# Reordering the first attention of a fused gated-attention and expert kernel, with the weight loads ahead, the state update later and each later gate two units ahead of its use

## The chip, the cores and the metric

One core of one Trainium2 chip. In the profiles PE is TensorE (PEld its weight loads), DVE is VectorE, ACT ScalarE, POOL GpSimd and SP SyncE; L142 is line 142 of the kernel. The metric is the device time of one execution in microseconds (us), median of several executions. The mean granted TensorE clock is recorded with each: I call span x granted clock the *full-clock time*. It is a calculation (it treats all time at half clock as half lost).

## The reference

```python
# gated linear attention: B=4, H=8, S=768, D=48
f = sigmoid(f_logit)
for t in range(S):
    state = f[t][:, None] * state + outer(k[t], v[t])
    y[t] = q[t] @ state
# then four experts for all tokens, x = y as (3072, 384)
p = domain_probs / domain_probs.sum(-1)
out = sum(p[:, e] * (relu(x @ w1[e]) @ w2[e]) for e in range(4))   # w1: 384x1024, w2: 1024x384
```

## The kernel before

The sequence is cut into 6 chunks of 128 steps. A chunk's attention, for 4 batches, runs `gate` (ACT), `pe_cs` (cumulative sums on TensorE), `exps` (ACT, then q and k products on DVE and POOL), `pe_tp`/`ev_tp` (transposes and copy), `pe_at`/`ev_at` (scores and mask), `pe_y`/`ev_y`, `pe_kv`/`ev_kv`/`state` (the recurrent state for the next chunk) and `pe_xt`/`ev_xt` (the experts' input). The expert work is cut into *units*: `mm_h`, three matmuls of the first product (L286), and `mm_o`, four of the second (L302). Chunk c+1's attention is issued between chunk c's units; chunk 0's has nothing beside it. Each engine takes its instructions in program order, and the program order is what the author writes.

```python
gate(0, 0)
plan = staggered(attention_plan(0))        # steps of batch b at 5*b + s
nw = [(0, 1), (1, 1), (0, 2), (2, 1), (1, 2), (3, 1), (2, 2), (3, 2)]   # (expert, w1 or w2)
for s in sorted(plan):
    if s == 5: gate(0, 1)
    if s == 10:
        w_ins.append(load_w(*nw.pop(0)))   # POOL's queue; casts to bf16
        after(w_ins[0], kB)
    run_steps(plan[s])                     # PE part of a step, then its ACT/DVE/POOL part
for w in nw:                               # seven loads behind all of POOL's work
    w_ins.append(load_w(*w))
...
def state(c, b):                           # on POOL
    for r in range(2):
        nc.gpsimd.tensor_tensor(out=Sf[ps, b], in0=Sf[ps, b], in1=eg, op=ALU.mult)
        nc.gpsimd.tensor_copy(out=nb[ps, b, :, r * D:(r + 1) * D], in_=Sf[ps, b])
...
# inside chunk c >= 1: attention of chunk c+1, at these units
base = 4 if c > 1 else 20
for s, x in staggered(plan).items():
    steps.setdefault(base + s - 4, []).extend(x)
for half in range(2):                      # the gate stands at the same unit as the first sums
    steps.setdefault(base - 4 + half, []).insert(0, ([lambda half=half: gate(c + 1, half)], []))
```

## Time and profile before

| | before |
|---|---|
| median of 3 executions | 352.21 us (350.58 to 352.37) |
| profiled span, granted clock | 354.0 us, 0.975 |
| TensorE / DVE / ACT / POOL busy | 89 / 45 / 42 / 27 % |
| first expert matmul | 30.18 us |
| first second-product matmul | 42.03 us |

The page's view of the span in 40 slices of 8.9 us; each digit is a busy share or a clock in tenths:

```profile
PE   0677599988785999989999989999899999999995
PEclk9999989999697899999999999999999999999999
DMA  9962999999896049004069011000011000010002
```

TensorE is full from the sixth slice on but for a dent at 71 to 115 us (digits 8, 8, 7, 8, 5). The clock row dips in the sixth, eleventh, thirteenth and fourteenth slice. The transfer engines are busy until 115 us, but TensorE names a transfer as its reason for waiting only near 38 and 42 us. The rest is in the prediction.

### The profile page before, as it was taken

Reading aid. Unit: us, or ns where it says so; the run is one execution under the profiler, and the core shown is the slowest. Engines: PE = TensorE matmul, PEld = TensorE weight load, DVE = VectorE, ACT = ScalarE, POOL = GpSimd, SP = SyncE. Lnnn points to the kernel's source line nnn. Section 1 sums busy time; section 2 is a strip of 40 time slices with the busy share of each in tenths; the row PEclk is TensorE's granted clock in tenths of the full one; section 3 lists DMA queues with packets and bytes.
Section 4 is the critical chain, followed back from the end, with each engine's and each line's share of the span. In section 5 each row is a group of like instructions: output and inputs, shape, how many; then the busy total and the mean of one; then the engine's idle time right before and its main releaser. Section 6 shows DMA issues by size and latency. Waiting matters only on the chain.

```text
span 354.0 us, 5713 instructions
## 1 busy us (share of the span) xinstructions
PE 313.7 (89%) x2272; PEld 184.4 (52%) x2304; DVE 161.0 (45%) x259; ACT 149.0 (42%) x295; POOL 96.2 (27%) x164
## 2 busy tenths in 40 slices
PE   0677599988785999989999989999899999999995
PEld 0563245555463765545665545665455555555553
DVE  4574123437071466535456435456353463432343
ACT  4433243252546553373553464533455534234320
POOL 4458100053514471122441122442134300000000
PEclk9999989999697899999999999999999999999999
DMA  9962999999896049004069011000011000010002
GB/s 176 184 92 38 208 206 193 218 208 224 206 224 106 0 96 215 4 22 107 8 131 183 0 45 46 2 0 2 1 50 42 3 0 2 22 67 2 0 2 89
DMA packets 111403, 30.31 MB, mean 86 GB/s; under 512 B 102672, under 2 KB 109840, under 8 KB 111376
## 3 DMA queue, kind: packets, MB, share of 16 engines
q1 hardware_dynamic: 105616, 23.65, 34.4%
q0 software_dynamic: 5760, 6.29, 10.8%
q8 instruction: 18, 0.29, 0.3%
q14 instruction: 9, 0.07, 0.1%
HBM read 31.51 MB, written 4.72 MB: 102 GB/s over the span
## 4 chain that ended last, share of the span: by engine, by line
PE 78%; ACT 6%; DMA 4%; DVE 3%; POOL 3%; issue 3%; SPq 1%; ACTq 0%; POOLq 0%; DVEq 0%
PE op L302 34%; PE hp L286 32%; PE pt L176 3%; DMA w_sb<-in_moe_w_dram 3%; PE A L194 2%; ACT gp L135 2%; ACT ex L133 2%; DMA fg<-in_f_logit_dram 2%; PE pt L229 2%; DVE AT L200 1%; PE pt L142 1%; PE pt L215 1%; POOL kp L164 1%; ACT h_sb L294 1%; PE pt L255 1%
## 5 line engine op out<-in xcount | busy, mean ns | idle before, releaser
L286 PE MATMUL hp<-xT,w_sb 128*128 128x512 bf16 (+1 forms) x592 | 159.9, 374 | 6.4 <-ACT xT L261 1.7
L302 PE MATMUL op<-w_sb,h_sb 128*128 128x384 bf16 x768 | 156.4, 329 | 3.3 <-DMA w_sb<-in_moe_w_dram 3.1
L294 ACT ACTIVATE h_sb<-hp 128x512 bf16<-128x512 f32 (+1 forms) x130 | 73.3, 564 | 133.2 <-PE hp L286 125.2
L302 PEld LDWEIGHTS <-h_sb 128*128 128x128 bf16 x768 | 75.2, 99 | 70.5 <-issue 5.1
L292 DVE TENSOR_SCALAR h_sb<-hp 128x512 bf16<-128x512 f32 (+1 forms) x78 | 50.7, 650 | 81.9 <-PE hp L286 80.0
L286 PEld LDWEIGHTS <-w_sb 128*128 128x128 bf16 x624 | 58.3, 101 | 50.0 <-issue 11.3
L312 DVE SCALAR_TENSOR_TENSOR o_sb<-op,pn,o_sb 128x384 f32<-128x384 f32 x72 | 44.4, 617 | 64.1 <-PE op L302 56.4
L162 POOL TENSOR_TENSOR qp<-qg,eQ 128x384 bf16<-128x384 f32 x20 | 20.0, 998 | 120.6 <-ACT eQ L153 89.2
L247 POOL TENSOR_TENSOR Sf<-Sf,egs 48x192 f32<-48x192 f32 x40 | 20.1, 502 | 52.6 <-DVE Sf L239 50.9
L200 DVE TENSOR_TENSOR AT<-A,mask 128x1024 bf16<-128x1024 f32 x24 | 29.3, 1222 | 3.0 <-PE A L194 2.4
L164 POOL TENSOR_TENSOR kp<-kg,eK 128x384 bf16<-128x384 f32 x24 | 24.7, 1030 | 10.1 <-ACT egs L159 10.1
L239 DVE TENSOR_TENSOR Sf<-Sf,pt 48x192 f32<-48x192 f32 x40 | 14.0, 351 | 22.6 <-PE pt L229 19.6
L142 PE MATMUL pt<-gp,Ub 128*128 128x384 bf16 x24 | 9.0, 374 | 15.3 <-ACT gp L135 15.3
L309 ACT ACTIVATE o_sb<-op,pn 128x384 f32<-128x384 f32 x24 | 14.0, 584 | 15.5 <-PE op L302 14.8
L183 DVE COPY QK<-pt 112x1024 bf16<-112x1024 bf16 x24 | 16.5, 689 | 8.5 <-PE pt L176 8.5
L221 ACT CAST yb<-pt 128x384 bf16<-128x384 f32 x24 | 11.6, 483 | 15.9 <-PE pt L215 15.6
L153 ACT ACTIVATE eQ<-pt 128x384 f32<-128x384 f32 x24 | 11.7, 488 | 12.9 <-PE pt L145 11.9
L261 ACT COPY xT<-pt 128x384 bf16<-128x384 bf16 x24 | 11.4, 477 | 12.7 <-PE pt L255 12.7
L145 PEld LDWEIGHTS <-gp 128*112 128x112 bf16 x80 | 8.9, 158 | 14.5 <-issue 12.8
L248 POOL CAST sb<-Sf 48x192 bf16<-48x192 f32 x40 | 13.6, 340 | 2.6
L215 PE MATMUL pt<-vb,AT 128*128 128x48 bf16 x192 | 11.9, 190 | 2.5 <-DVE AT L200 1.3
L176 PE MATMUL pt<-ident,qp 128*112 128x128 bf16 x96 | 10.6, 240 | 3.5 <-DVE qp L162 2.5
(45 smaller groups left out, 179.4 us busy)
## 6 DMA issues: line engine op xcount, KB each, us to landing
w_sb<-in_moe_w_dram POOLq DMA_DIRECT2D x8, 768.0 KB, 14.2
fg<-in_f_logit_dram SPq DMA_DIRECT2D x12, 384.0 KB, 5.8
kg<-in_k_dram SPq DMA_DIRECT2D x12, 384.0 KB, 5.6
qg<-in_q_dram SPq DMA_DIRECT2D x12, 384.0 KB, 5.8
vg<-in_v_dram SPq DMA_DIRECT2D x12, 384.0 KB, 5.6
out_dram<-o_sb SPq DMA_DIRECT2D x24, 192.0 KB, 1.9
pt<-in_moe_domain_probs_dram SPq DMA_DIRECT2D x1, 48.0 KB, 9.9
```

What stands on the lines that cost most here:

```text
L162: lead.tensor_tensor(out=Qpad[c % NB][:, b, :, 0:D], in0=t["q"][:, bs, :], in1=eQ.rearrange("t (h d) -> t h d", d=D), op=ALU.mult)
L164: nc.gpsimd.tensor_tensor(out=Kpad[c % NB][:, b, :, 0:D], in0=t["k"][:, bs, :], in1=eK.rearrange("t (h d) -> t h d", d=D), op=ALU.mult)
L176: nc.tensor.transpose(out=tp[:, j, i, :], in_=src[:, b, 2 * i:2 * i + 2, :].rearrange("t h d -> t (h d)")[:, 0:MP], identity=ident)
L183: nc.vector.tensor_copy(out=QK, in_=t["tp", b])
L200: nc.vector.tensor_tensor(out=AT.rearrange("s r i t -> s (r i t)"), in0=t["A", b].rearrange("s r i t -> s (r i t)"), in1=mask01, op=ALU.mult)
L215: nc.tensor.matmul(out=y[:, h * D:(h + 1) * D], lhsT=AT[:, r, i, :], rhs=vb[:, h, :], start=(c == 0), stop=True, skip_group_check=True)
L247: nc.gpsimd.tensor_tensor(out=Sf[ps, b], in0=Sf[ps, b], in1=eg, op=ALU.mult)
L286: nc.tensor.matmul(out=hp[:, n0:n1], lhsT=w1_sb[:, e, kk, fc * 128:(fc + 1) * 128], rhs=t["xT"][:, kk, n0:n1], start=(kk == 0), stop=(kk = ...
L292: nc.vector.tensor_relu(out=hs[:, fc, n0:n1], in_=hp[:, n0:n1])
L294: nc.scalar.activation(out=hs[:, fc, n0:n1], in_=hp[:, n0:n1], func=AF.Relu)
L302: nc.tensor.matmul(out=op, lhsT=t["h", e][:, fc, nt * T:(nt + 1) * T], rhs=w2_sb[:, e, fc, :], start=(fc == 0), stop=(fc == KF - 1))
L312: nc.vector.scalar_tensor_tensor(out=o, in0=op, scalar=pe, in1=o, op0=ALU.mult, op1=ALU.add)
```

## The change

It means to shorten the one attention that has nothing beside it (steps issued batch by batch in the order in which a pipeline would run them, inputs loaded by quarter), to have the weights in place in time (all eight on POOL's queue right behind its last key product), to keep chunk 0's state update off that path (issued at expert units 3, 5, 7 and 9), and to leave two units between a later chunk's gate and its first use. Small moves in PSUM, where TensorE's results go, come with it (chunk 0's sums and expert-input transposes take banks that the experts use later).

```diff
-    load(0, 0, "fkq")
-    load(0, 1, "f")
...
+    for x in "f0 k0 q0 f1 f2 k1 q1 v0 f3 k2 q2 v1 k3 q3 v2 v3".split():
+        ins = load(0, x[0], int(x[1]), int(x[1]) + 1)
...
-            if c < C - 1:
+            if 0 < c < C - 1:
                 pe.append(lambda b=b: pe_kv(c, b))
...
+    def first_attention():
+        for b in range(B):
+            for at, f in ((0.0, gate), (1.2, pe_cs), (1.8, exps), (3.0, products), (4.2, pe_tp),   # (abridged)
+                          (5.4, ev_tp), (6.2, pe_at), (6.9, ev_at), (7.0, cast_v), (8.2, pe_y),
+                          (8.8, ev_y), (9.4, pe_xt), (10.0, ev_xt)):
+                ops.append((3.6 * b + at, b, f))
+            if b == B - 1:
+                ops.append((3.6 * b + 4.1, b, weights))
+        for at, b, f in sorted(ops, key=lambda x: x[:2]):
+            f()
...
-                        steps.setdefault(min(30 + 2 * i + b, n), []).append(plan[b, s])
+                        steps.setdefault(min(31 + 2 * i + b, n), []).append(plan[b, s])
+                for b in range(B):
+                    steps.setdefault(3 + 2 * b, []).append(
+                        ([lambda b=b: pe_kv(0, b)], [lambda b=b: ev_kv(0, b), lambda b=b: state(0, b)]))
...
-                base = 4 if c > 1 else 20
+                base = 2 if c > 1 else 18
-                    steps.setdefault(base + s - 4, []).extend(x)
+                    steps.setdefault(base + s, []).extend(x)
```

More of the change, by code (lines that the diff above doesn't have):

```diff
@@ L61, with load @@
     cur = {}
-    def load(c, half, names):
+    def load(c, names, b0, b1):
         t = cur.setdefault(c, {})
@@ L68, in load @@
                 t[nm] = io.tile([T, B * H, D], FP32, name=nm + "g")
-            hs = slice(half * 16, half * 16 + 16)
+            hs = slice(b0 * H, b1 * H)
             ins.append(nc.sync.dma_start(out=t[nm][:, hs, :], in_=srcs[nm][c, :, hs, :]))
@@ L76, in after @@
                           reason="order of transfers")
-    load(0, 0, "fkq")
-    load(0, 1, "f")
-    load(0, 0, "v")
-    kB = load(0, 1, "kqv")[0]
+    for x in "f0 k0 q0 f1 f2 k1 q1 v0 f3 k2 q2 v1 k3 q3 v2 v3".split():
+        ins = load(0, x[0], int(x[1]), int(x[1]) + 1)
+        if x == "k3":
+            k_last = ins[0]
     pt = const.tile([128, B * C, E], FP32)
@@ L125, in load_w, with bank, gate @@
         return nc.gpsimd.dma_start(out=w2_sb[:, e], in_=w2_r[e])
-    def gate(c, half):
+    def bank(c, kind, shape, dtype):
+        if c == 0 and kind == "cs":
+            return ps_h.tile(shape, dtype, name="hp")
+        if c == 0 and kind == "xp":
+            return ps_o.tile(shape, dtype, name="op")
+        return ps_t.tile(shape, dtype, name="pt")
+    def gate(c, b0, b1):
         t = cur[c]
-        hs = slice(half * 16, half * 16 + 16)
-        ex = wk.tile([T, 16, D], FP32, name="ex")
+        hs = slice(b0 * H, b1 * H)
+        ex = wk.tile([T, 16, D], FP32, name="ex")[:, 0:(b1 - b0) * H]
         nc.scalar.activation(out=ex, in_=t["f"][:, hs, :], func=AF.Exp, scale=-1.0)
@@ L139, in pe_cs @@
         g = Gpad[c % NB]
-        cs = ps_t.tile([T, 512], FP32, name="pt")
+        cs = bank(c, "cs", [T, 512], FP32)
         t["cs", b] = cs
@@ L155, in exps @@
         nc.scalar.activation(out=eK, in_=cs[:, 0:HD], func=AF.Exp)
+        t["e", b] = (eQ, eK)
         if c < C - 1:
@@ L159, in exps, with products @@
             nc.scalar.activation(out=t["egs"][:, b, :], in_=cs[0:MP, HD:HD + NP], func=AF.Exp, scale=-1.0)
+    def products(c, b):
+        t = cur[c]
+        eQ, eK = t["e", b]
         bs = slice(b * H, b * H + H)
@@ L165, in exps, with cast_v @@
                                 in1=eK.rearrange("t (h d) -> t h d", d=D), op=ALU.mult)
-        vb = wk.tile([T, H, D], BF16, name="vb")
+    def cast_v(c, b):
+        t = cur[c]
+        bs = slice(b * H, b * H + H)
+        lead = nc.vector if c == 0 else nc.gpsimd
+        vb = wk.tile([T, H, D], BF16, name="vb", bufs=5)
         lead.tensor_copy(out=vb, in_=t["v"][:, bs, :])
@@ L171, in pe_tp @@
         t = cur[c]
-        tp = ps_t.tile([MP, 2, NP, T], BF16, name="pt")
+        tp = bank(c, "tp", [MP, 2, NP, T], BF16)
         t["tp", b] = tp
@@ L205, in pe_y @@
         t = cur[c]
-        y = ps_t.tile([T, 512], FP32, name="pt")
+        y = bank(c, "y", [T, 512], FP32)
         t["y", b] = y
@@ L225, in pe_kv @@
         t = cur[c]
-        KV = ps_t.tile([T, 512], FP32, name="pt")
+        KV = bank(c, "KV", [T, 512], FP32)
         t["KV", b] = KV
@@ L251, in pe_xt @@
         t = cur[c]
-        xp = ps_t.tile([T, KD, T], BF16, name="pt")
+        xp = bank(c, "xp", [T, KD, T], BF16)
         t["xp", b] = xp
@@ L269, in attention_plan @@
             o = 0
-            put(o, [lambda b=b: pe_cs(c, b)], [lambda b=b: exps(c, b)])
+            put(o, [lambda b=b: pe_cs(c, b)], [lambda b=b: exps(c, b), lambda b=b: products(c, b), lambda b=b: cast_v(c, b)])
             put(o + 4, [lambda b=b: pe_tp(c, b)], [lambda b=b: ev_tp(c, b)])
@@ L361, in run_steps, with weights @@
                 x()
-    gate(0, 0)
-    plan = staggered(attention_plan(0))
-    nw = [(0, 1), (1, 1), (0, 2), (2, 1), (1, 2), (3, 1), (2, 2), (3, 2)]
-    w_ins = []
-    for s in sorted(plan):
-        if s == 5:
-            gate(0, 1)
-        if s == 10:
-            w_ins.append(load_w(*nw.pop(0)))
-            after(w_ins[0], kB)
-        run_steps(plan[s])
-    for w in nw:
-        w_ins.append(load_w(*w))
+    def first_attention():
+        ops = []
+        for b in range(B):
+            for at, f in ((0.0, lambda b=b: gate(0, b, b + 1)), (1.2, lambda b=b: pe_cs(0, b)),
+                          (1.8, lambda b=b: exps(0, b)), (3.0, lambda b=b: products(0, b)),
+                          (4.2, lambda b=b: pe_tp(0, b)), (5.4, lambda b=b: ev_tp(0, b)),
+                          (6.2, lambda b=b: pe_at(0, b)), (6.9, lambda b=b: ev_at(0, b)),
+                          (7.0, lambda b=b: cast_v(0, b)), (8.2, lambda b=b: pe_y(0, b)),
+                          (8.8, lambda b=b: ev_y(0, b)), (9.4, lambda b=b: pe_xt(0, b)),
+                          (10.0, lambda b=b: ev_xt(0, b))):
+                ops.append((3.6 * b + at, b, f))
[3 more added lines that the diff above has]
+            f()
+    w_ins = []
+    def weights():
+        for w in ((0, 1), (1, 1), (0, 2), (2, 1), (1, 2), (3, 1), (2, 2), (3, 2)):
+            w_ins.append(load_w(*w))
+        after(w_ins[0], k_last)
+    first_attention()
     pn = const.tile([128, B * C, E], FP32)
@@ L382 @@
     nc.vector.tensor_tensor(out=pn, in0=pt, in1=psm.broadcast_to([128, B * C, E]), op=ALU.mult)
-    l1 = load(1, 0, "fkqv")
+    l1 = load(1, "fkqv", 0, 2)
     after(l1[0], w_ins[5])
-    load(1, 1, "fkqv")
-    load(2, 0, "fqkv")
-    load(2, 1, "fqkv")
+    load(1, "fkqv", 2, 4)
+    load(2, "fkqv", 0, 2)
+    load(2, "fkqv", 2, 4)
     for c in range(C):
@@ L400 @@
                     for b in (0, 1):
-                        steps.setdefault(min(30 + 2 * i + b, n), []).append(plan[b, s])
-                steps.setdefault(29, []).append(([lambda: gate(1, 0)], []))
+                        steps.setdefault(min(31 + 2 * i + b, n), []).append(plan[b, s])
+                steps.setdefault(29, []).append(([lambda: gate(1, 0, 2)], []))
+                for b in range(B):
+                    steps.setdefault(3 + 2 * b, []).append(
+                        ([lambda b=b: pe_kv(0, b)], [lambda b=b: ev_kv(0, b), lambda b=b: state(0, b)]))
             else:
-                base = 4 if c > 1 else 20
+                base = 2 if c > 1 else 18
                 for s, x in staggered(plan).items():
-                    steps.setdefault(base + s - 4, []).extend(x)
+                    steps.setdefault(base + s, []).extend(x)
                 for half in range(2):
-                    steps.setdefault(base - 4 + half, []).insert(0, ([lambda half=half: gate(c + 1, half)], []))
+                    steps.setdefault(base - 2 + half, []).insert(
+                        0, ([lambda half=half: gate(c + 1, 2 * half, 2 * half + 2)], []))
             if c == 1:
@@ L413 @@
                         steps.setdefault(min(at + b - 2, 15), []).append(plan[b, s])
-                steps.setdefault(2, []).append(([lambda: gate(1, 1)], []))
+                steps.setdefault(2, []).append(([lambda: gate(1, 2, 4)], []))
         for i, (h, o) in enumerate(us):
             if i == 0 and 1 <= c and c + 2 < C:
-                load(c + 2, 0, "fqkv")
-                load(c + 2, 1, "fqkv")
+                load(c + 2, "fkqv", 0, 2)
+                load(c + 2, "fkqv", 2, 4)
             if h:
```

## The prediction

> **What bounds the kernel now.** I read the page first. TensorE (PE) is 89% busy, and the chain that ended last is 78% PE (34% line L302, the second expert product; 32% L286, the first), so most of the span is a saturated PE and only its idle stretches can be won. The busy table by stretches, cut where the stages change, says where these are:
>
> ```profile
> core 0: us, PE busy (x) PEld busy (x) DVE busy (x) ACT busy (x) POOL busy (x), PEclk, DMA share, GB/s
> 0.00:30.18 30.18, 14.93 (x145) 11.95 (x145) 18.31 (x35) 11.99 (x25) 14.83 (x31) 1.00 0.85 132
> 30.18:42.03 11.85, 7.65 (x27) 2.82 (x27) 2.90 (x5) 3.58 (x6) 6.84 (x10) 1.00 0.89 144
> 42.03:72.90 30.87, 30.71 (x155) 15.94 (x158) 10.16 (x16) 11.20 (x19) 0.00 (x0) 0.94 1.21 207
> 72.90:86.92 14.02, 11.57 (x121) 7.45 (x119) 8.33 (x14) 4.73 (x12) 7.30 (x13) 1.00 1.20 215
> 86.92:126.36 39.44, 31.58 (x288) 22.80 (x288) 14.65 (x27) 21.15 (x51) 17.43 (x28) 0.83 0.69 130
> 126.36:354.04 227.68, 217.26 (x1541) 123.41 (x1568) 106.66 (x164) 96.35 (x184) 49.84 (x84) 1.00 0.19 44
> ```
>
> The first attention takes 30.18 us before the first expert matmul, with no engine full (PE 14.9, DVE 18.3, POOL 14.8): a latency chain. Then PE works 7.65 of 11.85 us. The later loss is small per us. The chain of waits around the second row says what holds it:
>
> ```profile
> 28.94 0.36 DVE Sf L239
> ...
> 30.44 0.51 POOL Sf L247
> 30.96 0.05 issue
> 31.01 0.34 POOL sb L248
> 31.35 0.74 POOL w_sb L124
> 32.09 9.89 DMA w_sb<-in_moe_w_dram
> 41.99 0.04 issue
> 42.03 0.81 PE op L302 x4
> ```
>
> Seven of the eight weight loads stand on POOL's in-order queue behind the last batch's state update (L247, L248); they are issued from 31.3 us, and the first L302 matmul waits until 42.03. PE's own waits after 30.18 us:
>
> ```profile
> PE pt L142 <- ACT gp L135: 9.1, 6, 2.1
> PE op L302 <- DMA w_sb<-in_moe_w_dram: 3.1, 1, 3.1
> PE hp L286 <- ACT xT L261: 1.7, 3, 0.6
> ```
>
> The largest, 9.1 us in six pieces, is not in the first attention: it is the cumulative-sum matmul (L142) of a later chunk, issued right behind its gate (L133, L135 on ACT). Three of them, 1.69 us each at 153.9, 205.3 and 256.7 us in the timeline, are the only PE waits the view names after 120 us. Last, the half-clock stretches:
>
> ```profile
> 42.85:46.26 3.41, 3.41 (x10) 1.37 (x9) 0.69 (x1) 0.58 (x1) 0.00 (x0) 0.50 1.17 206
> 90.63:97.46 6.83, 6.32 (x33) 4.20 (x32) 0.85 (x2) 2.95 (x10) 4.76 (x6) 0.50 0.76 199
> 111.11:117.94 6.83, 5.47 (x36) 3.78 (x36) 1.55 (x4) 4.05 (x11) 3.43 (x5) 0.50 0.28 58
> ```
>
> The PEclk column is 0.50: each follows a stretch in which PE stood idle a lot.
>
> **What the Trainium skill says.** (1) "TensorE: Matmul & The Clock Gate", Part 1: the array's clock is halved after an idle window of about 3.4 us and restored after a busy one, and windows run free of the program. The trace agrees: the slow stretches are 3.41 and 6.83 us, one and two such windows, behind windows with at most about half of PE busy (1.65 of 3.43 us before 90.63, 1.20 of 3.40 before 111.11). (2) Same page, "Architectural detail": ACT, DVE and POOL queues are strict FIFO. The trace agrees: weight loads 2 to 8, with nothing of their own to wait for, are issued only after the last L248. (3) "DMA: Bandwidth & Descriptors", "Issuing engines are not separate DMA queues": loads from SP and POOL share the same 16 engines. The trace agrees: the chunk-1 loads, beside the last two weights, took 11.2 us to land against 5.8 in the median. (4) "SBUF — State Buffer", "Who interferes with whom": DVE and POOL share a port pair, the loser blocks. One L164 product took 1.80 us beside DVE work against 1.0 usually; I allow for some of this.
>
> **The change, part by part.**
>
> *Loads by batch.* 384 KB halves land 1.8 us apart (8.3, 10.1, 11.9 us ...), so 192 KB quarters should land 0.9 us apart: f0 at about 3.5 instead of 4.4, the last k at 14.3, the last v at 17.0. The bytes are the same. Gain about 0.9 us at the start.
>
> *First attention step by step.* I walk it through in-order queues in the new order with the trace's durations: gate 1.0 us per batch (two of 0.49), L142+L145 0.85, each exp 0.49, qp 0.7, kp 1.0, transposes 1.1, QK copy 0.69, A 0.61, mask product 1.23, v cast 0.36, y 0.50, yb 0.49, xT transposes 0.50, xT copy 0.48. One batch alone takes nearly 10 us. ACT needs 3.1 us per batch and DVE 3.0 (3.7 with the state's 0.73, now gone), but order waits between them spread the batches to about 4.2 us. The walk gives gates ending at 4.5, 7.5, 11.0 and 15.8, kp of the last batch at 19.6, and the last xT at 26.7. **First L286 at about 26.8 instead of 30.18: -3.4 us.**
>
> *Weights.* They now stand on POOL right after that kp: issued from 19.6 to 26.4 us (8 x 0.85). The first load of an idle queue took 6.8 us (31.3 to 38.1), then one landed every 3.85 us (38.1, 42.0, 45.7, 49.5, 53.2). So w1[0] lands at 26.4, in time (it is issued later than before, 14.4, and landed at 22.7, so this slack is spent), w1[1] 30.2, w2[0] 34.1, w1[2] 38.0. PE: 24 L286 matmuls from 26.8, about 3.4 us of them at half clock (0.43 us each, then 0.22), are 6.9 us; the state's key-value products, now among them, 4 x 0.25 us more; one further group of 0.65. First L302 at about 35.2, after w2[0]. **The waits for weights, 3.1 + 0.7 us, vanish, and the half clock at 42.85, which costs 3.41/2 = 1.7 us, has no cause any more.** The first L302 moves from 42.03 to 35.2, 6.8 us, and with the clock the end of that stage is about 8.5 us earlier. I take -8.2 for small waits on the hp buffers, since the deferred adds give DVE 4 x 0.73 us just there.
>
> *Later attention 2 units after its gate instead of at it.* A unit is 1.30 us (one L286 group and one L302 half), so two cover the gate's 1.7 us: 3 x 1.69 = **-5.1 us**, taken as -4.8. In chunk 1 the units at that place are half-width L286 alone (0.33 us each) and ACT has two gates (3.4 us) anyway: PE then runs into the hp buffers that ACT must clear, so of 2.08 us there I give only -1.0.
>
> *Chunk 0 to 1.* The first two batches' steps start one unit later (31 for 30). The chain from their L142 at 73.4 to the first L286 of chunk 1 at 86.9 is 13.5 us of latency (POOL products 4 x 1.0 + 2 x 0.5, then the masks one after the other), and one unit less stands beside it: +1.3 less the 0.34 us of gate wait gone, **about +0.7**. The inputs follow the weights, so they move 9 us earlier too, and the loads do not become the limit.
>
> Sum: -8.2 - 4.8 - 1.0 + 0.7 = -13.3 us. From 352.2 that is 338.9. The half clock at 90.6 and 111.1 costs up to 3.4 us each; the first has its cause unchanged, the second may go or move (I give it one chance in three: -1.1). **Predicted 338 us.**
>
> **Rivals.** (a) *The weights become the wait at the start.* w1[0] has 0.4 us of slack by the estimate. If POOL writes its load commands slowly beside DVE, or the last inputs and the tiny probability load overlap it, PE waits 1 to 3 us at 26.8 and again at w2[0]: 339 to 342. Against it: the loads took 0.74 to 0.93 us to issue in every case. (b) *The pipeline of the first attention does not shorten*, because in-order queues block each other (A has one buffer, ACT has 11 instructions per batch): the start stays near 30 us, but the weights are still 11 us ahead, so the stall and the clock loss still go: about 341. (c) *The gate wait only changes its name*: ACT is no faster, and PE waits for relu results instead (as at 113.27 us, 1.30 us on L294). In full-width chunks ACT ends gate 2 about 3.5 us after gate 1 begins, just as PE comes to need the buffer; if half is given back: 340.5. (d) *The clock decides*: with fewer idle stretches both later slow stretches vanish: 333; if phases fall badly: 342.
>
> **Range and chances.** The three gains (start 3.4, weights and clock 5, gates 5) come from separate mechanisms, each seen as a wait in the trace; for a change under 2% (above 345.2) two of the three would have to fail. The errors: start +-2, weights +-2, clock +-3, gates +-2, together about +-5. Range 332 to 344; faster 0.95, same 0.05, slower under 0.01.
>
> **What would show it.** First L286 near 26.8 us and the weight issues near 19.6 to 26.4; no PE wait on w_sb over 1 us; no half clock between 35 and 60 us; the wait of L142 on L135 down from 9.1 us to under 4, with none after 120 us; the stretch from the chunk-1 L142 to its first L286 still about 13.5 us. The prediction is wrong if PE waits for L294 or w_sb as much as it did for L135 and w_sb before, or if the first L286 stays at 30 us.

## The result, and the profile after

The changed kernel takes **338.66 us** (336.81 to 339.08, 4 executions) against 352.29 us (350.58 to 356.76, 4 executions) for the kernel before. The ratio is 0.9618, 95% interval 0.9572 to 0.9665 (a ratio is the mean time of one kernel's fast runs over that of the other's of the same rounds, so not quite the ratio of the medians quoted). The predicted 338 was 0.7 us off.

In the changed kernel the first product is L304, the second L320, the sums L150, the gate L141 and L143. Its stretches, cut at the same events as the prediction's first table (columns as there: length, busy us of TensorE matmul, weight load, DVE, ACT, POOL, then clock, transfer share, GB/s), with the stretch after the first second-product matmul cut at the start of the sums of chunk 1:

```profile
core 0: us, PE busy (x) PEld busy (x) DVE busy (x) ACT busy (x) POOL busy (x), PEclk, DMA share, GB/s
0.00:25.10 25.10, 13.80 (x129) 10.01 (x129) 15.67 (x29) 12.61 (x29) 14.34 (x24) 1.00 0.92 164
25.10:33.51 8.41, 8.36 (x40) 3.81 (x41) 4.00 (x9) 2.99 (x5) 2.89 (x7) 1.00 1.21 207
33.51:64.19 30.68, 30.68 (x170) 16.38 (x169) 11.32 (x19) 12.71 (x21) 3.85 (x10) 1.00 1.22 209
64.19:77.72 13.53, 10.63 (x115) 6.71 (x113) 8.01 (x13) 3.88 (x11) 6.99 (x12) 1.00 1.20 210
77.72:112.17 34.45, 26.98 (x274) 20.04 (x274) 13.39 (x26) 20.49 (x50) 16.19 (x26) 0.95 0.78 148
112.17:335.10 222.93, 219.04 (x1582) 124.26 (x1581) 107.07 (x165) 95.98 (x185) 51.54 (x88) 1.00 0.20 45
```

The first stretch is 5.1 us shorter. The second is 3.4 us shorter, and TensorE now works 8.36 of its 8.41 us: the weight stall is gone. From the first second-product matmul to chunk 1's first expert matmul it is 44.2 us (33.51 to 77.72) against 44.9 (42.03 to 86.92). Chunk 1 takes 34.5 us against 39.4, the rest 222.9 against 227.7. These sum to 18.9 us, more than the medians differ, because the profiled execution of the kernel before had a clock of 0.975 and that of the changed one 0.995, the best of its five. Chunk 1 shows it: the delay behind the gate is worth 0.8 of its 5.0 us (below), and most of the rest goes with the slow stretch at 90.63, which has no counterpart here. With the same chunk-1 code, the run "weights alone" below lacks that stretch and takes 36.59 us (82.39 to 118.98) where the kernel before takes 39.44.

The chain around the start, in order of time (start, us, what):

```profile
18.23 6.82 DMA w_sb<-in_moe_w_dram
25.05 0.05 issue
25.10 4.43 PE hp L304 x12
```

The first weight still ends the wait, as before the third one did; but the timeline has the last copy of the experts' input end at 24.87, so this costs only 0.2 us. TensorE's waits after 26 us:

```profile
PE pt L150 <- ACT gp L143: 2.8, 2, 1.6
PE A L212 <- DVE AT L218: 1.6, 2, 0.9
PE hp L304 <- ACT xT L279: 1.1, 2, 0.6
```

The wait on the gate has fallen from 9.1 to 2.8 us, and the same view from 120 us on names no wait at all.

### The profile page after: what moved, and what is told of

Its sections match the earlier page's. It is cut to its first block, busy times and chain, and to the rows that moved or that the text cites. A ratio compares the mean times of both kernels' runs of the same rounds, so it can differ in the third digit from the quotient of the medians.

```text
span 335.1 us, 5754 instructions
## 1 busy us (share of the span) xinstructions
PE 309.5 (92%) x2304; PEld 181.2 (54%) x2304; DVE 159.5 (48%) x259; ACT 148.7 (44%) x299; POOL 95.8 (29%) x164
## 4 chain that ended last, share of the span: by engine, by line
PE 86%; ACT 4%; DMA 3%; DVE 3%; POOL 3%; issue 1%; POOLq 0%; DVEq 0%; ACTq 0%
PE hp L304 38%; PE op L320 36%; PE pt L194 3%; DMA w_sb<-in_moe_w_dram 2%; PE A L212 2%; POOL kp L177 2%; PE pt L247 1%; PE pt L233 1%; PE pt L229 1%; PE pt L150 1%; PE pt L273 1%; ACT eQ L161 1%; DVE Sf L257 1%; ACT ex L141 1%; DMA fg<-in_f_logit_dram 1%
## 5 line engine op out<-in xcount | busy, mean ns | idle before, releaser
L304 PE MATMUL hp<-xT,w_sb 128*128 128x512 bf16 (+1 forms) x624 | 159.5, 368 | 4.4 <-ACT xT L279 1.1
L320 PE MATMUL op<-w_sb,h_sb 128*128 128x384 bf16 x768 | 154.9, 326 | 0.0
L320 PEld LDWEIGHTS <-h_sb 128*128 128x128 bf16 x768 | 74.7, 98 | 65.9
L304 PEld LDWEIGHTS <-w_sb 128*128 128x128 bf16 x624 | 57.0, 100 | 45.3 <-issue 7.2
L201 DVE COPY QK<-pt 112x1024 bf16<-112x1024 bf16 x24 | 16.6, 690 | 21.8 <-PE pt L194 21.8
L257 DVE TENSOR_TENSOR Sf<-Sf,pt 48x192 f32<-48x192 f32 x40 | 14.1, 352 | 15.4 <-PE pt L247 14.6
L279 ACT COPY xT<-pt 128x384 bf16<-128x384 bf16 x20 | 9.5, 477 | 22.5 <-PE pt L273 22.5
L161 ACT ACTIVATE eQ<-pt 128x384 f32<-128x384 f32 x20 | 9.8, 490 | 15.4 <-PE pt L153 11.6
L194 PEld LDWEIGHTS <-qp 128*112 128x112 bf16 x96 | 9.4, 146 | 5.8 <-DVE qp L175 2.9
L194 PE MATMUL pt<-ident,kp 128*112 128x128 bf16 x96 | 10.8, 241 | 1.8 <-POOL kp L177 1.8
```

The costliest lines, as they stand in the source:

```text
L194: nc.tensor.transpose(out=tp[:, j, i, :], in_=src[:, b, 2 * i:2 * i + 2, :].rearrange("t h d -> t (h d)")[:, 0:MP], identity=ident)
L201: nc.vector.tensor_copy(out=QK, in_=t["tp", b])
L257: nc.vector.tensor_tensor(out=Sf[ps, b], in0=Sf[ps, b], in1=KV[ps, :, r, :], op=ALU.add)
L304: nc.tensor.matmul(out=hp[:, n0:n1], lhsT=w1_sb[:, e, kk, fc * 128:(fc + 1) * 128], rhs=t["xT"][:, kk, n0:n1], start=(kk == 0), stop=(kk = ...
L320: nc.tensor.matmul(out=op, lhsT=t["h", e][:, fc, nt * T:(nt + 1) * T], rhs=w2_sb[:, e, fc, :], start=(fc == 0), stop=(fc == KF - 1))
```

## The experiments

Eleven kernels and the changed one once more, all correct. The kernel before ran beside each group: its medians were 355.83 to 355.93 us on these chips, not 352, with a granted clock of 0.966 to 0.984. Its 21 executions in three groups span 352.1 to 357.2 us, but their full-clock time only 343.4 to 345.5, mean 344.8. The changed kernel's is 333.0 to 333.7, mean 333.4, in its first five executions. So I compare full-clock times ("full" below) beside medians. No 95% interval of a ratio below is wider than 0.0095 either way, and all lie below 1.

Full-clock time has two limits. It leaves in the slow first matmuls of the expert stage, at which PEclk says 1.00: the first twelve take 4.43 us in one profiled execution of the changed kernel and 5.10 in the other, so 0.37 to 0.43 us each, against 0.24 right after (1.46 for six). And it overrates half clock: of these two executions one has 3.4 us of it in chunk 1, the other 6.8, yet chunk 1 takes 34.45 and 34.92 us. So differences under about 1 us are better read from a stage. The last stage, from chunk 1's first full-width expert matmul on, is 222.9 us in all ten profiled runs with the delay and 227.7 in all four without.

### The delay behind the gate

**Undone in the changed kernel:**

```diff
-                base = 2 if c > 1 else 18
+                base = 0 if c > 1 else 16
...
-                    steps.setdefault(base - 2 + half, []).insert(
+                    steps.setdefault(base + half, []).insert(
```

> The changed kernel with one part undone: in chunks 1 to 4 the attention of the next chunk follows its gate at once again, not 2 units later. Theory (the delay hides the gate's 1.7 us behind two units of 1.30 us): PE's waits of the cumulative-sum matmul on the gate come back, three of about 1.7 us after 112 us and one of about 2 us in chunk 1 instead of 1.1; time about 5.5 us longer than the changed kernel, 344 us, ratio to the kernel before about 0.977. Rival (the wait only changes its name, ACT being no faster): under 2 us longer, 338.7 to 340.5, ratio 0.962 to 0.967, since in the changed kernel PE would wait for relu results instead.

Measured: 344.08 us, ratio 0.9675, full 338.0. Waits of TensorE after 125 us:

```profile
PE pt L150 <- ACT gp L143: 5.1, 3, 1.7
```

All three waits are back, at their old size. **Alone, in the kernel before:**

```diff
-                    steps.setdefault(base + s - 4, []).extend(x)
+                    steps.setdefault(base + s - 2, []).extend(x)
```

> The kernel BEFORE with one part of the change alone: in chunks 1 to 4 the next chunk's attention follows its gate by 2 units. Theory: the three gate waits of 1.69 us after 126 us vanish whatever happens at the start; the stretch from chunk 1's first full-width expert matmul to the end falls from 227.7 to 222.9 us; with the granted clock taken out (span times granted clock, 344.8 us for the kernel before) 339.5 to 340.5. Rival (the gain needs the rest of the change, or shows as another wait): under 2 us, 343 or more.

Measured: 350.40 us, ratio 0.9889, full 339.0; from chunk 1's first full-width expert matmul (125.64 us) to the end (348.6) it is 223.0 us against 227.7. The delay is worth 4.7 us in chunks 2 to 4 in either kernel, and no other wait takes its place there. In chunk 1 it is worth about 0.8 us (38.67 us from first expert matmul to first full-width one, against 39.44).

### What shortens the start

**Weights alone, in the kernel before:** all eight loads at step 15, behind the last key product.

```diff
-        if s == 10:
-            w_ins.append(load_w(*nw.pop(0)))
-            after(w_ins[0], kB)
         run_steps(plan[s])
-    for w in nw:
-        w_ins.append(load_w(*w))
+        if s == 15:
+            for w in nw:
+                w_ins.append(load_w(*w))
+            after(w_ins[0], kB)
```

> The kernel BEFORE with one part of the change alone: all eight weight loads are put on POOL's queue right behind the last batch's key product, ahead of the state updates that follow. Theory: issued from about 22.5 us; first weight lands at 29.3, just ahead of the first expert matmul at 30.2; third at 37; the first second-product matmul at about 38 instead of 42.0, and the half clock behind the old stall goes (1.7 us): 4.5 to 6 us shorter, 346.5 to 348, ratio 0.983 to 0.987. Rival (the gain of the change is the shorter first attention): within 2 us of the kernel before.

Measured: 347.97 us, ratio 0.9786, full 341.9. The first expert matmul stays at 30.05; the first second-product matmul comes at 39.2 instead of 42.0, and no half clock follows it. The queue position counts by itself: 2.9 us of full-clock time.

**Deferral alone, in the kernel before** (old step order, old loads; the value tile gets five buffers, as in the change):

```diff
-            if c < C - 1:
+            if 0 < c < C - 1:
                 pe.append(lambda b=b: pe_kv(c, b))
...
+                for b in range(B):
+                    steps.setdefault(3 + 2 * b, []).append(
+                        ([lambda b=b: pe_kv(0, b)], [lambda b=b: ev_kv(0, b), lambda b=b: state(0, b)]))
```

> The kernel BEFORE with one part of the change alone: the state work of chunk 0 is taken out of the first attention and put at units 3, 5, 7 and 9, in the old step order with the old half loads. Theory (the deferral by itself frees POOL's queue, as the weights moved alone did, and shortens the chain a little): weights 2 to 8 issued from 22.5 us; first expert matmul at 28 to 29.5 us instead of 30.2; first second-product matmul at 37 to 38; span times granted clock 340 to 341.5 against 344.8. Rival A (it is all there is to the gain at the start): first expert matmul at 25 to 26, 337 to 338. Rival B (only the queue matters): first expert matmul at 30, 341.9 as with the weights moved alone.

Measured: 345.36 us, ratio 0.9731, full 339.2. First expert matmul at 27.45 us, first second-product matmul at 36.7, both earlier than I expected. Loads 2 to 8 are issued from 21.0 us, right behind the last key product, because nothing else of POOL's is left:

```profile
20.09 1.00 POOL L164 TENSOR_TENSOR kp<-kg,eK 128x384 bf16<-128x384 f32 x1 [2.36 <-ACT egs L159]
21.03 0.80 POOL L124 DMA_DIRECT2D w_sb<-in_moe_w_dram  x1
```

This one part carries 5.6 of the 11.4 us of full-clock gain, and 2.7 of the 5.1 us at the start.

**State work put back into the new order**, right behind each batch's output, the weights left where they are (in this run and the next two, the lines that issue the deferred work at units 3 to 9 are taken out; cut here):

```diff
-                          (8.8, lambda b=b: ev_y(0, b)),
+                          (8.5, lambda b=b: pe_kv(0, b)), (8.8, lambda b=b: ev_y(0, b)),
+                          (8.9, lambda b=b: ev_kv(0, b)), (9.0, lambda b=b: state(0, b)),
...
```

> The changed kernel, but the key-value product, its adds and the state update of chunk 0 are back inside the first attention, right behind each batch's output; the weights keep their place on the queue. Theory (the deferral matters mainly through POOL's queue; two of the four updates still stand ahead of the weights, but in time that POOL has to spare): first expert matmul 1 to 3 us later (DVE has 0.73 us more per batch, PE 0.6), 1 us given back later because four groups of 0.25 us leave the expert stage: +0.5 to +2 us, 339 to 340.5 us. Rival (deferral is what shortens the pipeline): first expert matmul back near 30 us, +4 us or more, 343.

Measured: 343.38 us, ratio 0.9673, full 337.7, and the first expert matmul at 30.59 us: my theory was wrong and the rival right in size. The reason stands on DVE's queue. First this run, then the changed kernel, from the same place:

```profile
10.93 0.35 DVE L185 CAST vb<-vg 128x384 bf16<-128x384 f32 x1
12.96 0.74 DVE L257 TENSOR_TENSOR Sf<-Sf,pt 48x192 f32<-48x192 f32 x2 [1.68 <-PE pt L247]
13.73 0.69 DVE L201 COPY QK<-pt 112x1024 bf16<-112x1024 bf16 x1
```

```profile
11.09 0.35 DVE L185 CAST vb<-vg 128x384 bf16<-128x384 f32 x1
11.66 0.69 DVE L201 COPY QK<-pt 112x1024 bf16<-112x1024 bf16 x1 [0.23 <-PE pt L194]
```

The adds (L257) are 0.74 us of work, but DVE stands 1.68 us in front of them for a matmul that TensorE has behind the next batch's sums, and the next batch's copy (L201), whose input is ready, stands behind the adds. The spacing of the batches goes from 3.7 to 5.8 us (ends of the input copies: 13.8, 19.6, 25.3, 30.5). So I tested whether it is the work or its place, with the state work **behind the next batch's mask product**:

```diff
-                          (10.0, lambda b=b: ev_xt(0, b))):
+                          (10.0, lambda b=b: ev_xt(0, b)), (10.2, lambda b=b: pe_kv(0, b)),
+                          (11.0, lambda b=b: ev_kv(0, b)), (11.1, lambda b=b: state(0, b))):
...
```

> The changed kernel with chunk 0's key-value product, adds and state update in the first attention as in the earlier run of that kind, but placed behind the same batch's last copy and the next batch's mask product instead of ahead of the next batch's query-key copy. Theory (in that run the 0.73 us of adds cost 2 us per batch only because DVE waited, in order, for a matmul that stood behind the next batch's sums on PE, and held up the next copy): first expert matmul at 25.5 to 27.5 us instead of 30.6, and the time within 1.5 us of the changed kernel. Rival (the added work itself stretches the pipeline to 5.7 us per batch wherever it stands): first expert matmul at 29.5 or later, 343 us.

Measured: 340.90 us, ratio 0.9621, full 336.4. The last input copy now ends at 26.0 us (30.5 in the run before, 24.9 in the changed kernel): it is mostly the place. The time is 2.2 us above the changed kernel's 338.66, more than the 1.5 expected: the first expert matmul is at 28.5, later than my range, for another reason. POOL's queue and TensorE's wait:

```profile
20.77 0.50 POOL L265 TENSOR_TENSOR Sf<-Sf,egs 48x192 f32<-48x192 f32 x1
21.33 0.34 POOL L266 CAST sb<-Sf 48x192 bf16<-48x192 f32 x1
21.62 1.70 POOL L124 DMA_DIRECT2D w_sb<-in_moe_w_dram  x2
...
28.54 0.61 PE L304 MATMUL hp<-xT,w_sb 128*128 128x512 bf16 x1 [2.68 <-DMA w_sb<-in_moe_w_dram]
```

The state updates of the first two batches now stand in front of the loads. The second comes behind the last key product and waits 0.84 us for DVE, and the loads start at 21.6 instead of 18.2. The deferral frees two queues at once, DVE's and POOL's.

**Both put back**: the state work as in the first of these runs, and seven of the eight loads after the whole attention.

```diff
-                ops.append((3.6 * b + 4.1, b, weights))
+                ops.append((3.6 * b + 4.1, b, first_weight))
...
+    def first_weight():
+        w_ins.append(load_w(0, 1))
+        after(w_ins[0], k_last)
...
     first_attention()
+    weights()                 # the other seven
```

> The changed kernel with the state update back in the first attention AND seven of the eight weight loads behind it on the queue, as in the kernel before; only the order of the first attention, the quarter loads and the later delay stay changed. Theory (the queue position of the weights is worth about as much as the pipeline): last state update ends at 28 to 29 us, second weight lands at about 35.5, third at 39.5, so the first second-product matmul is at about 39.5 instead of 33.5 and a half-clock stretch can come back: +6 to +8 us on the changed kernel, 345 to 347. Rival (the weights hardly matter once the pipeline is shorter): within 2 us of the run with only the state put back.

Measured: 348.96 us, ratio 0.9800, full 340.4. The loads are issued from 31.45 us, right behind the last state cast, and the first second-product matmul is at 42.2, with a half clock at 43.1: the old stall, whole, and more than I had expected (39.5 and 345 to 347 us). The new order alone, with state and weights as they were (the state work at this place), gains nothing at the start: 30.3 and 42.2 us against 30.2 and 42.0.

**Weights written after the attention, state deferred:**

```diff
-            if b == B - 1:
-                ops.append((3.6 * b + 4.1, b, weights))
...
     first_attention()
+    weights()
```

> The changed kernel with the weight loads written after the whole first attention instead of ahead of the last batch's steps; the state update stays deferred. Theory (a place on a queue is worth only what stands in between, and with the state deferred POOL has nothing between the last key product and the end): same as the changed kernel within 0.5 us, weights issued at 18 to 19 us. Rival (the place in program order counts by itself): weights issued after 24 us, +6 us.

Measured: 338.48 us, ratio 0.9533, full 333.3; loads issued from 18.12 us. In its group the changed kernel itself ran again as a reference:

> The changed kernel itself once more, on the chip of the next three runs, as their reference: 338 to 339 us, ratio to the kernel before 0.957 to 0.967. If the share of half-clock time is what separates executions, each time less half of its half-clock time should agree within 0.5 us between executions.

Measured: 338.45 us, ratio 0.9532 (the kernel before was at 355.85 on this chip), loads from 18.07 us, full 332.9. The two are the same, as expected: once the state is deferred, nothing stands between, and the line in which the change writes the loads is worth nothing. The part of that expectation on the clock held less well: its four full-clock times span 332.1 to 333.3, not 0.5 us.

One thing these runs leave open. Deferral alone and delay alone already add up to the whole full-clock gain (5.6 and 5.8 of 11.4 us). The new order and the quarter loads bring the first expert matmul another 2.4 us forward (27.45 to 25.10), and the later start of chunk 1 gives 0.8 back (next section). No run has deferral and delay in the old order, nor the quarter loads or the PSUM moves by themselves, so what these are worth in the end is not shown.

### The unit at which chunk 1 begins

```diff
-                        steps.setdefault(min(31 + 2 * i + b, n), []).append(plan[b, s])
+                        steps.setdefault(min(30 + 2 * i + b, n), []).append(plan[b, s])
```

> The changed kernel with the first two batches of chunk 1 starting at unit 30 again instead of 31. Theory (from their first matmul to chunk 1's first expert matmul is a latency of 13.5 us in both kernels, so what starts a unit of 1.3 us earlier ends that much earlier, less the gate wait of 0.34 us): 0.7 to 1 us shorter than the changed kernel. Rival (the gate wait and a crowded ACT eat it): no difference within 0.4 us, or longer.

Measured: 339.04 us (336.19 to 341.06), ratio 0.9544, full 331.5. Inconclusive in time, and 1.4 us shorter in full-clock time than the changed kernel beside it (332.9). The stage agrees with the expectation instead: from the first second-product matmul to chunk 1's first expert matmul it is 43.40 us (34.36 to 77.76), against 44.23 (34.05 to 78.28) in the changed kernel on the same chip, 0.8 less. But the profiled execution loses more than that in chunk 1, 38.65 us against 34.92. Two of its four executions had a clock of 0.977, and the profiled one shows where (windows of TensorE's clock, this run, then the changed kernel, then the kernel before; columns as above):

```profile
78.11:81.52 3.41, 1.63 (x14) 1.05 (x12) 0.43 (x1) 2.61 (x5) 0.46 (x2) 1.00 1.31 248
81.53:88.36 6.83, 6.32 (x33) 4.08 (x32) 0.85 (x2) 2.91 (x9) 4.75 (x6) 0.50 0.58 149
```

```profile
76.29:79.70 3.41, 2.52 (x20) 1.58 (x19) 1.47 (x4) 1.79 (x5) 2.37 (x6) 1.00 1.28 215
79.70:83.11 3.41, 1.83 (x19) 1.48 (x19) 0.42 (x1) 3.02 (x8) 0.67 (x1) 1.00 1.20 312
96.77:100.18 3.41, 1.32 (x11) 0.88 (x11) 0.11 (x1) 3.38 (x7) 0.17 (x1) 1.00 1.32 218
```

```profile
87.22:90.63 3.41, 1.63 (x13) 1.04 (x12) 0.42 (x1) 2.57 (x5) 0.52 (x2) 1.00 1.34 229
```

The changed kernel's windows are counted back in steps of 3.41 us, the length of its one slow stretch, which began at 100.18. The same gap behind chunk 1's first gate (1.63 us in all three) falls inside one window in this run and in the kernel before (1.63 of 3.41 us busy, half clock follows), but in the changed kernel it is shared by two (2.52 and 1.83 busy, none follows). Why the windows lie as they do, no run shows. It is not the program alone: two of this kernel's own four executions had a clock of 0.990, like the changed kernel.

### A version that beats both

The windows table shows 2.9 us of idle TensorE in the 13.5 us before chunk 1, whose attention starts late in chunk 0. **Its first two batches earlier and spread over full units**, the last weight load behind the first half of chunk 1's inputs:

```diff
-                for i, s in enumerate((0, 4, 7, 11, 13)):
+                for s, at in ((0, 26), (4, 29), (7, 31), (11, 34), (13, 37)):
...
+                steps.setdefault(24, []).append(([lambda: gate(1, 0, 2)], []))
+                steps.setdefault(10, []).append(([lambda: after(load_w(3, 2), l1[3])], []))
```

> The changed kernel, with the attention of chunk 1's first two batches begun at unit 26 (gate at 24) and spread to unit 38, so that full units of the expert stage stand beside its latency; the last weight load waits for the first half of chunk 1's inputs so that these land in time. Theory (2.9 us of PE idle in the 13.5 us latency and the gaps before chunk 1's first expert matmul can be filled): chunk 1's first expert matmul at 73.5 to 75 us instead of 77.7, 3 to 4 us shorter than the changed kernel, 335. Rival (the inputs or the delayed last weight become the wait): PE waits for a load between 55 and 66 us and it is the same or longer.

Measured: 334.52 us, ratio 0.9433, full 329.9; chunk 1's first expert matmul at 74.4 us. Then **the second two batches' gate and sums in chunk 0 as well**:

```diff
+                steps.setdefault(34, []).append(([lambda: gate(1, 2, 4)], []))
+                for b in (2, 3):
+                    steps.setdefault(36 + b, []).append(plan[b, 0])
...
-                for s, at in ((0, 3), (4, 9), (7, 11), (11, 13), (13, 15)):
+                for s, at in ((4, 4), (7, 7), (11, 11), (13, 14)):
...
-                steps.setdefault(2, []).append(([lambda: gate(1, 2, 4)], []))
```

> The version with chunk 1's first two batches begun at unit 26, with the second two batches moved the same way: their gate at unit 34 of chunk 0 and their sums at units 38 and 39, so that chunk 1 does not begin with a gate wait of 1.63 us. Theory: that wait goes and ACT is free of 4 us in chunk 1's first half-width units; 1 to 3 us shorter than the version before it (334.5; span times granted clock 329.9), 332, and a half-clock stretch less in chunk 1. Rival (ACT and DVE are the limit there, whoever asks first): no gain, other waits of the same size in chunk 0's last units.

Measured: **332.25 us** (331.80 to 332.71), ratio 0.9372 (0.9305 to 0.9438), full 328.0. Its stretches from the first second-product matmul on:

```profile
33.89:75.33 41.44, 40.48 (x288) 23.66 (x291) 18.71 (x32) 18.66 (x35) 13.04 (x26) 1.00 1.15 204
75.33:108.08 32.75, 27.41 (x268) 20.24 (x267) 13.83 (x27) 18.15 (x47) 14.89 (x23) 0.90 0.93 179
```

TensorE idles under 1 us of 41.4 before chunk 1, and chunk 1 takes 32.8 us. The hope of one half-clock stretch less was not met in the profiled run: one of 6.8 us remains at 93.7 (chunk 1's clock is 0.90). This is the best version that I ran.

## Why the prediction was right, point by point

- **Weights and the stall: right.** The third load was to land at 34.1 and the stall to vanish; loads land at 25.05, 28.8, 32.7 and 36.4 us, and the second products start at 33.5 without a wait. The half clock at 42.85 is gone. Rival (a) is there, at 0.2 us instead of 1 to 3; it came out whole where state updates stood ahead of the loads (a wait of 2.68 us), and in the best version's profiled run there is one of 1.13.
- **The start: right in direction, mis-sized.** I wrote 26.8 us (-3.4); it is 25.1 (-5.1). The term that failed is the spacing of 4.2 us per batch; it is 3.6 (input copies end at 13.94, 17.65, 21.00 and 24.87). Part of it is that I had added full durations on DVE: 0.7 for the query product, 1.23 for the mask product. In the trace the query product takes 0.56 us (13.16) and the next instruction starts 0.49 after it, the one after the mask product 1.14 after it (13.65 to 14.79). That makes 2.67 us of DVE work in the batch from 11.09 to 14.79, where I had 3.0. The other 1.03 us of its 3.70 are waits, for which my 4.2 left 1.2. In a dependent chain one adds durations; for the work in a queue one takes start-to-start times.
- **The cause of the start: named too loosely.** I put it down to the order of steps and the quarter loads and mentioned the state only as 0.73 us of DVE. Deferral alone brings 2.7 of the 5.1 us, and the new order with the state left beside each output brings none (first expert matmul at 30.3 and 30.6): that is rival (b), which the deferral held off. What the two do together is to keep adds that wait for a late matmul from holding up a copy that is ready.
- **The delay behind the gate: right, to 0.1 us**: -4.8 predicted for chunks 2 to 4, -4.75 measured (227.68 to 222.93). Rival (c) fails there and shows in part in chunk 1: with the delay undone the gate wait there is 3.7 us and TensorE's waits for relu results 1.5, with it 2.8 and 2.0. I had cut the gain there to 1.0; alone it was 0.8.
- **Chunk 0 to 1: the latency of 13.5 us was right** (13.53 measured). So was its price, +0.7: with unit 30 back, this stage is 0.8 us shorter, though no gain in the whole time was shown.
- **The clock: wrong in detail.** "The first has its cause unchanged": the cause is still there, the half clock at that place is not. Over the executions with a recorded clock, half clock costs at most (span x (1 - clock)) 5.6 to 12.1 us before, mean 8.3, and 1.7 to 5.1 after. Rival (d) is thus part of the result: 11.4 us of the gain is full-clock time, and on a chip where the kernel before ran at 355.9 us the ratio was 0.953 instead of 0.962.
- **The sum: close by luck.** I read the stages from the profiled execution, which took 355.75 us, and subtracted their gains from the median of 352.2. Between the two profiled executions the time fell by 18.9 us where my sum has 14.4. The way to the first second-product matmul gave 8.5 us for 6.8, chunk 1 gave 5.0 for 2.1 (mostly its clock); the other two stages agree to 0.1 us. A base that was 3.5 us too low nearly made up for the 4.5 us of gain that I had not foreseen.

## What to carry to other kernels

Look at what stands on each in-order queue in front of the instruction that is late: 0.74 us of adds cost 2 us per batch, most of it because of their place, and seven weight loads cost 3 us because state updates stood before them. Work that nobody needs soon belongs behind work that somebody waits for, and a producer's wait (here a 1.7 us gate) can be covered by putting work between it and its first use (here two full units, 2.6 us). Before you compare versions that differ by 1%, take out the granted clock: most of the spread of this kernel was there. Better still, compare the traces stage by stage: the last stage agreed to 0.1 us in all ten runs that had the same code there.

## What the Trainium skill lacked or had wrong

- "TensorE: Matmul & The Clock Gate", Part 1, speaks of one idle window, and its last part of gaps over about 3 us. Here half clock followed windows that were busy 1.63 and 1.32 of 3.41 us, with no single gap over 2.1 us, and did not follow windows busy 1.83 and 2.52. The page gives no busy share at which it happens.
- The same page says in Part 1 that the ramp penalty is under 1% of a typical kernel span. That is the start alone. Half clock later on is worth more here: one slow stretch of 6.8 us early in chunk 1 goes with 2.9 us (39.44 against 36.59 with the same chunk-1 code) or 3.7 us (38.65 against 34.92), about 1% by itself, and not every execution of a kernel has it.
- No page says that the profile's clock leaves out the slow start: PEclk is 1.00 while the first twelve expert matmuls take 0.37 to 0.43 us each, against 0.24 right after.
- "DMA: Bandwidth & Descriptors", Anatomy of one DMA: its fit for loads from POOL's queue does not say which bytes count when the load casts. One weight (1.57 MB read as fp32, half of it written as bf16) took 6.8 us from issue to landing on an idle queue (others were issued behind it), where the fit gives 5.6 us for the bytes read, and the next four landed 3.7 to 3.9 us apart.
